# One recurrent layer and two feed-forward layers on one core: six expert units chosen from 13 tiles, then a straight list of units or the general ones

## The chip, the cores and the metric

One core of one Trainium2 chip runs the whole program; seven cores are idle. The time is the device time of one execution in microseconds (us), the median of the runs shown. Beside it stands one profiled execution with a trace of every instruction on the engines: TensorE (PE, its weight loads PEld), VectorE (DVE), ScalarE (ACT), GpSimd (POOL), and SyncE (SP), which here only issues DMAs.

## The reference

Three stages follow each other (batch 4, 8 heads, 768 steps, head size 40, so 3072 tokens of 320 numbers):

```python
# 1 mLSTM per head, with gates i, f and a sigmoid gate o
C = f_stab*C + i_stab*v k^T;  n = f_stab*n + i_stab*k
y = sigmoid(o) * (C q) / max(|n.q|, 1)
# 2 dense feed-forward, d_ff 1024
h = x @ w_in;  u = h*softmax(h);  x = layernorm(u)*g_ln @ w_out
# 3 mixture of 8 experts, one expert per token
logits = x @ w_gate + modality_bias[modality_id]; e = argmax(logits)
out = softmax(logits)[e] * (relu(x @ w1[e]) @ w2[e])      # w1 320x1024, w2 1024x320
```

The routing of the given inputs follows from the reference alone: expert 2 gets 1454 tokens, expert 4 gets 1545, expert 0 gets 73, the others none. Of the first 13 tiles of 128 tokens in the kernel's order, 803 tokens go to expert 2 and 827 to expert 4.

## The kernel before, in words

The tokens are cut into 24 tiles of 128 (chunk c of batch b). A step is a small function that issues the instructions of one thing for one tile: `score`, `pmul`, `mix_x` and their neighbours are the recurrent layer in chunks; `xs_p` and `xs_e` turn a tile's result; `ff_mm` multiplies by `w_in` into one PSUM tile `h` (a single buffer of two banks); `ff_max`, `ff_exp`, `ff_u`, `ff_sq`, `ff_r`, `ff_y`, `ff_yl` are the softmax gate and the norm; `proj` multiplies by `w_out` and the gate weights; `rows` writes the tile's 128 rows to a DRAM table. `r1a`, `r1b`, `r2`, `r3` route a group of tiles: small VectorE operations, a rank by matmul (`rk`), and one indirect DMA per tile that puts the token numbers into the lists of their experts.

The lists are cut into units. A full unit is 256 tokens of one expert, a half unit at most 128. `table_a`, `table_w`, `table_get`, `table_b` choose the expert and list rows of the next units on the chip. For unit j, `fetch_w j 0` and `fetch_w j 1` gather the expert's f32 weights (1.57 and 1.31 MB) into one of two staging sets (j mod 2); where unit j-2 had the same expert the gather's rows are out of bounds and nothing moves, though the instruction is still issued. `stat_a`, `stat_d`, `scale`, `scale2` find a scale from the sum of squares; `s1h`, `s1l`, `s2h`, `s2l` split the scaled weights into high and low f16 halves in one of two sets `w16` (j mod 2). `fetch_x` gathers and transposes the tokens; `h j 0..3` are 64 matmuls (`hp`) in four quarters, each followed by `hh` on ScalarE and `hl` on VectorE; `po j 0..1` are 48 matmuls; `ob` scales and scatters 128 rows to the output. `hs`, `hsh`, `hsl` are the same for a half unit. Every unit goes through stat, scale and split, also where the expert is that of unit j-2.

The order of the work is written out by hand: `MAIN` is one list of steps, and each engine issues its part in exactly that order, so an engine that waits holds all that stands behind it. `MAIN` ends within unit 2 and the preparation of units 3 to 5. Two units are chosen when 18 tiles are routed, two when 22 are, the rest at the end. From unit 3 on the lists `PAIR`, `HALF`, `HALF_AHEAD`, `LAST_PAIR` and `LAST_HALF` are played for each unit; from unit 8 on they stand in nested `tc.If` blocks over two counts read from SBUF into registers. There PE, ACT and DVE are in written order, POOL and SP are ordered by the framework. For these inputs there are 12 full units (six of expert 2, then six of expert 4) and two halves.

Of the kernel before, what the change touches and what calls it, by code (L numbers as in the profile page):

```python
# [48 lines left out]
def _steps(text):  # L49
    steps = [step.split() for step in text.split(",")]  # L50
    return [(name, *map(int, args)) for name, *args in steps]

# [42 lines left out]
    mix_c 11, xs_e 8, load_ea 12, scale_q 12, ff_sq 7, ff_r 7, load_a 14, proj 6, rows 6, score 13, pmul 13 0,  # L95
    ff_y 7, ff_yl 7, k_t 15, k_e 15, norm_t 9, norm_d 9, r1b 0, decay 14, norm_x 9, load_ea 13, decay_c 13,
    mix_e 11, pmul 13 1, scale_v 13, ff_mm 8 0, ff_mm 8 1, ff_max 8, ff_exp 8, mix_c 10, load_kv 17, r2 0,
    proj 7, load_a 15, xs_p 9, ff_u 8, decay_exp 14, load_kv 16, score 14, decay_c 12, mix_x 12, rows 7,
    xs_e 9, ff_mm 9 0, ff_sq 8, ff_r 8, ff_y 8, decay_c 14, ff_yl 8, scale_v 14, mix_c 14, ff_mm 9 1, ff_max 9,
    scale_q 13, ff_exp 9, scale_v 12, mix_c 12, pmul 14 0, mix_c 13, decay 15, ff_u 9, r3 0, load_a 16, k_t 16,  # L100
    k_e 16, pmul 14 1, norm_t 10, norm_d 10, proj 8, mix_e 12, mix_x 13, score 15, ff_sq 9, ff_r 9, load_kv 18,
    rows 8, decay_exp 15, scale_v 15, load_ea 15, norm_x 10, xs_p 10, load_a 17, ff_y 9, pmul 15 0, ff_yl 9,
    k_t 17, k_e 17, norm_t 11, decay 16, xs_e 10, ff_mm 10 0, ff_mm 10 1, norm_d 11, mix_e 13, pmul 15 1,
    norm_x 11, ff_max 10, decay_exp 16, load_ea 18, do_sig 2, xs_p 11, xs_e 11, decay_c 15, scale_q 15,
    ff_exp 10, mix_x 14, load_ea 17, scale_v 16, mix_c 15, score 16, ff_u 10, ff_sq 10, decay 17, pmul 16 0,
    pmul 16 1, k_t 18, k_e 18, ff_r 10, load_ea 16, load_kv 19, proj 9, rows 9, decay_c 18, ff_y 10,
    decay_c 16, ff_yl 10, norm_t 12, norm_d 12, ff_mm 11 0, ff_mm 11 1, ff_max 11, norm_x 12, decay_c 17,
    mix_e 14, mix_x 15, load_a 18, decay_exp 17, scale_v 17, scale_q 17, score 17, ff_exp 11, ff_u 11, k_t 19,
    k_e 19, pmul 17 0, ff_sq 11, ff_r 11, xs_p 12, proj 10, xs_e 12, load_kv 20, ff_y 11, ff_yl 11, scale_q 16,
    load_a 19, rows 10, decay 18, norm_t 13, norm_d 13, norm_x 13, ff_mm 12 0, ff_mm 12 1, ff_max 12, mix_e 15,  # L110
    mix_x 16, pmul 17 1, mix_c 16, ff_exp 12, ff_u 12, decay_exp 18, scale_v 18, score 18, pmul 18 0, ff_sq 12,
    load_kv 21, pmul 18 1, xs_p 13, xs_e 13, scale_q 18, k_t 20, decay 19, k_e 20, ff_r 12, proj 11, rows 11,
    norm_t 14, norm_d 14, norm_x 14, ff_y 12, ff_yl 12, ff_mm 13 0, ff_mm 13 1, ff_max 13, xs_p 14, mix_c 17,
    load_a 20, mix_e 16, mix_x 17, decay_c 3, decay_exp 19, scale_v 19, xs_e 14, score 19, k_t 21, ff_exp 13,
    ff_u 13, proj 12, decay 20, pmul 19 0, pmul 19 1, ff_sq 13, ff_r 13, r1a 1, decay_c 21, k_e 21, load_kv 22,
    norm_t 15, ff_y 13, rows 12, load_ea 19, ff_yl 13, load_a 21, ff_mm 14 0, mix_e 17, norm_d 15, load_ea 20,
    ff_mm 14 1, ff_max 14, decay_exp 20, norm_x 15, score 20, mix_x 18, pmul 20 0, decay_c 23, scale_q 19,
    ff_exp 14, ff_u 14, mix_c 18, load_kv 23, pmul 20 1, decay 21, xs_p 15, xs_e 15, proj 13, ff_sq 14,
    ff_r 14, ff_mm 15 0, k_t 22, scale_q 20, rows 13, ff_y 14, ff_mm 15 1, mix_c 21, r1b 1, k_e 22, ff_yl 14,
    ff_max 15, norm_t 16, score 21, mix_e 18, norm_d 16, norm_x 16, ff_exp 15, mix_x 19, decay_exp 21,  # L120
    load_a 22, ff_u 15, load_sig 3, decay 22, pmul 21 0, xs_p 16, pmul 21 1, ff_sq 15, ff_r 15, k_t 23,
    xs_e 16, proj 14, ff_y 15, k_e 23, ff_yl 15, rows 14, norm_t 17, norm_d 17, ff_mm 16 0, mix_e 19, r2 1,
    norm_x 17, ff_mm 16 1, ff_max 16, norm_t 18, xs_p 17, do_sig 3, norm_d 18, norm_x 18, ff_exp 16,
    load_ea 21, xs_e 17, load_ea 22, proj 15, rows 15, load_a 23, norm_t 19, norm_d 19, scale_q 21, norm_x 19,
    decay_exp 22, mix_x 20, score 22, ff_u 16, pmul 22 0, pmul 22 1, scale_q 22, mix_e 20, norm_t 20,
    norm_d 20, ff_sq 16, ff_r 16, mix_x 21, mix_e 21, decay 23, norm_x 20, ff_mm 17 0, ff_y 16, ff_yl 16,
    norm_t 21, norm_d 21, decay_c 19, ff_mm 17 1, ff_max 17, xs_p 18, norm_x 21, xs_e 18, ff_exp 17, ff_u 17,
    r3 1, mix_x 22, mix_e 22, mix_c 19, decay_exp 23, score 23, pmul 23 0, xs_p 19, ff_sq 17, pmul 23 1,
    ff_mm 18 0, ff_mm 18 1, load_ea 23, scale_q 23, ff_r 17, xs_e 19, ff_max 18, ff_y 17, ff_exp 18, ff_yl 17,
    proj 16, ff_u 18, rows 16, ff_sq 18, xs_p 20, ff_mm 19 0, ff_r 18, ff_y 18, r1a 2, ff_yl 18, proj 17,  # L130
    rows 17, ff_mm 19 1, ff_max 19, decay_c 20, mix_x 23, mix_e 23, ff_exp 19, r1b 2, ff_u 19, norm_t 22,
    norm_d 22, proj 18, scale_q 3, xs_e 20, ff_mm 20 0, rows 18, r2 2, ff_mm 20 1, ff_sq 19, ff_r 19,
    ff_max 20, norm_x 22, xs_p 21, xs_e 21, ff_exp 20, ff_u 20, norm_t 23, ff_y 19, ff_yl 19, r3 2, ff_mm 21 0,
    ff_sq 20, ff_mm 21 1, ff_r 20, table_a 0, table_w 0, fetch_w 0 1, ff_max 21, norm_d 23, ff_y 20, ff_exp 21,
    ff_yl 20, fetch_w 0 0, xs_p 22, ff_u 21, xs_e 22, norm_x 23, ff_sq 21, ff_r 21, ff_mm 22 0, table_get 0,
    a_close, stat_a 0 1, fetch_w 1 0, r1a 3, ff_mm 22 1, ff_max 22, xs_p 23, decay_c 2, xs_e 23, mix_c 20,
    proj 19, stat_d 0 1, stat_d 0 0, ff_exp 22, stat_a 0 0, table_b 0, scale 0, ff_y 21, ff_yl 21, fetch_x 0,
    fetch_x 1, rows 19, s2h 0 1, s2l 0 1, scale2 0, s1h 0 2, s1l 0 2, s1h 0 0, s1h 0 1, ff_u 22, s2h 0 0,
# [1157 lines left out]
```

## Time and profile before

| | us |
|---|---|
| median of 3 runs (666.19, 670.79, 671.93) | 670.79 |
| profiled execution, its own time | 671.24 |
| span from its first to its last instruction | 669.4 |

| engine | busy us | share of the span | instructions |
|---|---|---|---|
| PE | 541.0 | 81% | 4367 |
| DVE | 514.4 | 77% | 1097 |
| ACT | 373.2 | 56% | 570 |
| POOL | 362.8 | 54% | 334 |

The span has three stretches: the recurrent and feed-forward tiles together (until about 361 us), the last feed-forward tiles alone (until about 414 us), and the expert units. A row of the timeline is: start in us, length in us, engine, line, operation, output tile <- input tiles, count; in brackets the idle time of the engine before it and what ended it.

### The profile page before, as it was taken

The numbers are of one execution on the slowest core, as the hardware profiler recorded it, in microseconds if no ns is written. First come the engines' busy times: TensorE is split into PE (matmuls) and PEld (weight loads), VectorE is DVE, ScalarE is ACT, GpSimd is POOL, SyncE is SP. The second block draws the span as 40 slices with busy tenths as digits, with TensorE's granted clock in tenths as the row PEclk, the third lists the DMA queues.
The fourth block names the chain that finished last, engine by engine and source line by source line (L and its number), as shares of the span: only waits on it lengthen the run. The fifth ranks groups of instructions, "written<-read, shape, count | busy, mean of one in ns | idle before, by whom it ended". The sixth has DMA issues, their size and how long they took to land.

```text
span 669.4 us, 12026 instructions
## 1 busy us (share of the span) xinstructions
PE 541.0 (81%) x4367; PEld 422.5 (63%) x4367; DVE 514.4 (77%) x1097; ACT 373.2 (56%) x570; POOL 362.8 (54%) x334
## 2 busy tenths in 40 slices
...
GB/s 216 143 215 158 162 203 14 136 171 153 186 166 156 99 193 171 131 151 181 92 64 45 207 240 125 52 83 56 104 111 254 189 60 51 84 213 87 69 13 2
DMA packets 126261, 87.07 MB, mean 130 GB/s; under 512 B 106415, under 2 KB 113177, under 8 KB 124904
## 3 DMA queue, kind: packets, MB, share of 16 engines
...
q10 hardware_dynamic: 1584, 5.77, 3.0%
...
## 4 chain that ended last, share of the span: by engine, by line
PE 33%; DVE 25%; DMA 14%; ACT 11%; issue 9%; POOL 5%; DVEq 0%; ACTq 0%; POOLq 0%
PE h L683 7%; DMA out<-ob,idc 5%; DMA stg<-in_wx,wii 4%; DVE w L1077 4%; ACT w L1070 3%; PE hp L1113 3%; PE xt L596 3%; PE s L575 2%; DMA raw<-in_w_out 2%; PE dp L529 2%; DVE w L1093 2%; DVE jkd L1048 2%; PE xt L600 2%; DVE yl L725 2%; PE po L739 2%
## 5 line engine op out<-in xcount | busy, mean ns | idle before, releaser
L1113 PE MATMUL hp<-xT,w 128*128 128x256 f16 x768 | 94.6, 285 | 1.6 <-DVE w L1077 1.6
L1113 PEld LDWEIGHTS <-w 128*128 128x128 f16 x768 | 78.7, 104 | 14.5 <-DVE w L1077 2.1
L683 PE MATMUL h<-win,xh 128*128 128x512 f32 x240 | 73.1, 438 | 7.1 <-DVE e L698 6.4
L1077 DVE SCALAR_TENSOR_TENSOR w<-stg,esc,w 128x1024 f16<-128x1024 f32 (+1 forms) x42 | 65.7, 1571 | 4.8 <-ACT w L1070 3.7
L1159 PE MATMUL po<-w,hl 128*128 128x320 f16 x192 | 57.5, 299 | 9.2 <-DVE hl L1125 9.0
L1070 ACT ACTIVATE w<-stg,esc 128x1024 f16<-128x1024 f32 x42 | 47.2, 1142 | 23.7 <-DVE esc L233 23.7
L739 PE MATMUL po<-woh,yhT 128*128 128x328 f16 x192 | 55.4, 309 | 4.9 <-DVE rowb L753 3.0
L683 PEld LDWEIGHTS h<-win,xh 128*128 128x128 f32 x240 | 47.1, 207 | 18.9 <-issue 6.4
L1158 PE MATMUL po<-w,hh 128*128 128x320 f16 x192 | 57.4, 299 | 1.7 <-POOL w L1099 1.6
L1157 PE MATMUL po<-w,hh 128*128 128x320 f16 x192 | 57.5, 300 | 0.1
L642 POOL TENSOR_TENSOR sig<-sig,den 128x320 f32<-128x320 f32 x24 | 20.4, 851 | 65.1 <-DVE den L640 57.6
L740 PE MATMUL po<-wol,yhT 128*128 128x328 f16 x192 | 55.3, 308 | 0.0
L1165 POOL DMA_INDIRECT out<-ob,idc x26 | 37.1, 1427 | 30.9 <-ACT ob L1164 16.0
...
L692 ACT ACTIVATE e<-h,nm 128x1024 f32<-128x1024 f32 x24 | 26.7, 1113 | 39.7 <-DVE nm L688 39.6
L542 POOL TENSOR_TENSOR abc<-abc,gcol 128x1024 f32<-128x1024 f32 x20 | 38.5, 1926 | 16.5 <-DMA abc<-a_dram 16.5
L1005 POOL DMA_INDIRECT stg<-in_wx,wii x30 | 36.1, 1202 | 20.7 <-ACT jka L1044 3.8
...
L1044 ACT ACTIVATE jka<-stg 128x2048 bf16<-128x2048 f32 (+1 forms) x24 | 40.7, 1694 | 7.0 <-DMA stg<-in_wx,wii 6.7
L683 PE MATMUL h<-win,xl 128*128 128x512 f32 x144 | 44.4, 419 | 0.1
L596 PE MATMUL xt<-p,va 128*41 128x128 f32 x384 | 40.8, 304 | 1.9 <-DVE p L582 1.7
L725 DVE SCALAR_TENSOR_TENSOR yl<-e,r_a,yh 128x1024 f16<-128x1024 f32 x24 | 37.3, 1555 | 5.8 <-ACT yh L718 5.8
...
## 6 DMA issues: line engine op xcount, KB each, us to landing
...
```

Source lines behind the costliest of these rows:

```text
L596: nc.tensor.matmul(xt[64 * par:64 * par + VA, j, :], va[:, 4 * par + j, :], p[:, 4 * par + j, :], start=True, stop=(c == 0))
L683: nc.tensor.matmul(h[:, f, :], xx[0:kk], win[0:kk, k, f * 512:(f + 1) * 512], start=(i == 0), stop=(i == 7))
L725: nc.vector.scalar_tensor_tensor(out=yl, in0=u_t.pop(n), scalar=r_a[:, n:n + 1], in1=yh, op0=ALU.mult, op1=ALU.subtract)
L739: nc.tensor.matmul(o, yhT[:, c, :], woh[:, c, :], start=(c == 0), stop=False)
L740: nc.tensor.matmul(o, yhT[:, c, :], wol[:, c, :], start=False, stop=False)
L1044: nc.scalar.activation(jk[0], st[:, 0:hw], AF.Square, accum_out=wsq[:, q, 0:1])
L1070: nc.scalar.activation(w[:, fs], st[:, fs], AF.Copy, scale=xbuf("esc", j, [128, 2], F32)[:, 0:1])
L1077: nc.vector.scalar_tensor_tensor(out=w[r, o], in0=st[r, fs], scalar=xbuf("esc", j, [128, 2], F32)[r, 0:1], in1=w[r, fs], op0=ALU.mult, op1 ...
L1113: nc.tensor.matmul(hp[:, f, :], w[0:kk, k * FF + fc * 128:k * FF + fc * 128 + 128], xT[0:kk, xk, :], start=(i == 0), stop=(i == 7))
L1157: nc.tensor.matmul(pq[:, 0:DM], th[:, fc, us], wh, start=(fc == 0), stop=False)
L1158: nc.tensor.matmul(pq[:, 0:DM], th[:, fc, us], wl, start=False, stop=False)
L1159: nc.tensor.matmul(pq[:, 0:DM], tl[:, fc, us], wh, start=False, stop=(fc == 7))
```

## The change

- `groups` (the tiles that are routed together) is 7, 6, 7 and 4 tiles in place of 7, 7, 4, 4, 2. `r1a 0`, `r1b 0`, `r2 0`, `r3 0` stand in a row behind `rows 6`; before, `r1a 0` stood ahead of `proj 5` and the three others were spread over the next three tiles.
- A new `table_f`, after 13 tiles are routed, takes the lowest and the highest expert that have at least 768 tokens by then, and makes units 0 to 5 of them in turn (low, high, low, high, low, high). `table_a 1` makes the other units (up to 19) at unit 3, again in turn from the front and the back of the list of full units, and `table_w` works out `go`: 1 if units 6 to 11 and 13 each have the expert of unit j-2, there are exactly six full units left and eight units in all.
- `MAIN` now holds units 0 to 5 whole. Weights are fetched and split for units 0 and 1 alone; for the others `scale3` applies the scale already found. In units 0 to 5 all four quarters of `h` take their PSUM tile from the two of `ps_h`.
- Then `go` is read into a register on every engine. Where it is 1, the list `TAIL` follows, without further branches and in written order on all five engines: units 6 to 11 without fetch or split, unit 12 fetched and split beside them, unit 13 before unit 12. Otherwise `READY` (fetch and split unit 6, fetch unit 7) and the units of before follow from unit 6.

The diff, cut to its core (in the two lists, all that concerns the units from the last tiles on):

```diff
-NPAIR = 12 + 7
-EARLY = (2, 2)
+NFAST = 6
+NREST = 12 + 7
+NPAIR = NFAST + NREST
...
-    xs_e 7, ff_sq 6, ff_r 6, r1a 0, load_kv 15, load_ea 14, ... proj 6, rows 6, score 13, pmul 13 0, ...
-    norm_d 9, r1b 0, decay 14, ... load_kv 17, r2 0, proj 7, ... ff_u 9, r3 0, load_a 16,
+    xs_e 7, ff_sq 6, ff_r 6, load_kv 15, load_ea 14, ... proj 6, rows 6, r1a 0, r1b 0, r2 0, r3 0, score 13,
...
+    r1a 1, c_units, r1b 1, score 20, ... r2 1, ff_max 14, k_t 22, table_f 0, ... table_get 0, ... table_b 0, ...
+    fetch_w 0 0, ff_sq 16, ... proj 18, rows 18, fetch_w 0 1, ff_mm 20 0,
+    ff_mm 20 1, ff_y 19, ff_yl 19, ff_max 20, norm_t 23, norm_d 23, xs_p 21, xs_e 21, norm_x 23, a_close,
+    fetch_w 1 0, ff_exp 20, ff_u 20, stat_d 0 0, xs_p 22, ff_mm 21 0, ff_mm 21 1, xs_e 22, stat_d 0 1,
+    decay_c 23, stat_a 0 1, ff_sq 20, ff_r 20, proj 19, stat_a 0 0, ff_y 20, ff_max 21, ff_yl 20, ff_exp 21,
+    ff_u 21, fetch_x 0, xs_p 23, rows 19, ff_sq 21, r1b 2, xs_e 23, stat_a 1 0, ff_mm 22 0, ff_r 21, ff_y 21,
+    ff_mm 22 1, ff_max 22, ff_yl 21, ff_exp 22, ff_u 22, fetch_x 1, proj 20, rows 20, ff_sq 22, scale 0,
+    ff_mm 23 0, s1h 0 1, ff_r 22, ff_y 22, r2 2, ff_mm 23 1, ff_max 23, ff_exp 23, s1l 0 1, ff_yl 22, proj 21,
+    rows 21, stat_d 1 0, s1h 0 2, s1h 0 0, s1l 0 0, fetch_w 1 1, s1l 0 2, h 0 0, stat_d 1 1, ff_u 23, s2h 0 1,
+    s2l 0 1, stat_a 1 1, ff_sq 23, ff_r 23, hh 0 0, hl 0 0, h 0 2, scale 1, ff_y 23, ff_yl 23, h 0 3, scale2 1,
+    hh 0 3, hl 0 3, s1h 1 1, s1l 1 1, proj 22, s2h 0 0, s1h 1 0, rows 22, h 0 1, hh 0 1, hl 0 1, s2h 1 1,
+    scale2 0, hh 0 2, proj 23, s2l 0 0, rows 23, hl 0 2, po 0 0, s1l 1 0, scale3 4, s1h 1 2, s1l 1 2, ob 0 0,
+    s2h 1 0, po 0 1, s2l 1 1, fetch_x 2, scale3 3, ob 0 1, h 1 0, hh 1 0, hl 1 0, h 1 1, hh 1 1, hl 1 1,
+    s2l 1 0, h 1 3, hh 1 3, hl 1 3, h 1 2, hh 1 2, hl 1 2, r3 2, po 1 0, ob 1 0, fetch_x 3, r1a 3, po 1 1,
+    ob 1 1, scale3 2, h 2 0, r1b 3, r2 3, r3 3, h 2 1, hh 2 0, hl 2 0, ...
+    po 3 0, table_a 1, ob 3 0, h 4 0, hh 4 0, po 3 1, hl 4 0, table_w 1, table_get 1, ob 3 1, h 4 1, table_b 1, ...
+TAIL = _steps("""
+    scale3 8, h 6 3, scale3 9, h 6 0, scale3 6, hh 6 0, h 6 1, hh 6 1, scale3 7, hh 6 3, hl 6 0, fetch_w 12 1,
+    hl 6 1, h 6 2, hh 6 2, hl 6 2, fetch_w 12 0, hl 6 3, po 6 0, ob 6 0, fetch_x 8, po 6 1, ob 6 1, h 7 0, ...
+    po 11 1, ob 11 1, s2l 12 0, hs 13 0, hs 13 1, hsh 13 0, hsl 13 0, hsh 13 1, hsl 13 1, s1h 12 0,
+    s1l 12 0, scale3 13, po 13 0, ob 13 0, hs 12 0, hs 12 1, hsh 12 0, hsl 12 0, hsh 12 1, hsl 12 1, po 12 0,
+    ob 12 0
+""")
...
+    def scale3(j):
+        einv = xbuf("einv", j, [128, 2], F32)
+        nc.vector.tensor_scalar(out=P2["gat"][:, 2 * j:2 * j + 2], in0=P2["gat"][:, 2 * j:2 * j + 2],
+                                scalar1=einv[:, 0:1], scalar2=einv[:, 1:2], op0=ALU.mult, op1=ALU.mult)
...
-        if f2 < 2 or j < 2:
+        if f2 < 2 or j < NFAST:
             hp = P2['ps_h'].tile([128, 2, 256], F32, tag="hp", name=f"hp{j}_{f2}")
...
+    play(MAIN)
+    at = saved()
+    straight = nc.values_load(P2["go"][0:1, 0:1], min_val=0, max_val=1)
+    with tc.If(straight > 0) as cmp:
+        play(TAIL)
+    with cmp.Else():
+        restore(at)
+        general(NFAST)
```

## Rows read from the trace of the kernel before

**Rows 1.** Page, part 1: busy us (share of the span) and instructions of each engine.

```profile
PE 541.0 (81%) x4367; PEld 422.5 (63%) x4367; DVE 514.4 (77%) x1097; ACT 373.2 (56%) x570; POOL 362.8 (54%) x334
```

**Rows 2.** Windows: stretch, length, then busy us of PE, PEld, DVE, ACT, POOL, granted clock, DMA.

```profile
250.00:300.00 50.00, 47.42 (x440) 37.83 (x436) 42.45 (x98) 23.82 (x40) 25.08 (x25) 1.00 0.69 156
...
540.00:560.00 20.00, 17.98 (x146) 13.83 (x144) 19.02 (x25) 17.05 (x20) 12.73 (x9) 1.00 0.27 62
```

**Rows 3.** Groups by line, DVE, 500 to 600 us (busy us, mean ns | idle before).

```profile
L1077 DVE SCALAR_TENSOR_TENSOR w<-stg,esc,w 128x1024 f16<-128x1024 f32 (+1 forms) x19 | 32.2, 1693 | 2.8 <-ACT w L1070 2.1
L1093 DVE SCALAR_TENSOR_TENSOR w<-stg,esc,w 128x1792 f16<-128x1792 f32 x7 | 18.7, 2675 | 0.0
L1125 DVE SCALAR_TENSOR_TENSOR hl<-hp,hh 128x512 f16<-128x512 f32 x27 | 18.6, 687 | 1.0
L1048 DVE SCALAR_TENSOR_TENSOR jkd<-stg 128x1024 bf16<-128x1024 f32 x12 | 16.1, 1341 | 0.2
```

**Rows 4.** Timeline, PE, unit stage: unit 3's first quarter, unit 3's second `po` matmul on.

```profile
480.58 2.00 PE L1113 MATMUL hp<-xT,w 128*128 128x256 f16 x16
...
492.56 0.30 PE L1158 MATMUL po<-w,hh 128*128 128x320 f16 x1 [1.58 <-POOL w L1099]
...
498.94 1.91 PE L1113 MATMUL hp<-xT,w 128*128 128x256 f16 x16
...
500.84 5.40 PE L1113 MATMUL hp<-xT,w 128*128 128x256 f16 x48
...
628.03 1.99 PE L1135 MATMUL hs<-xT,w 128*128 128x128 f16 x32 [1.00 <-SPq L1230]
```

**Rows 5.** Timeline, PE, from the end of `ff_mm 20` to unit 1.

```profile
360.26 0.87 PE L683 MATMUL h<-win,xl 128*128 128x512 f32 x3
...
387.99 0.40 PE L1000 MATMUL pi<-ident,idg 4*128 4x4 f32 x2 [3.44 <-DVE idg L997]
...
392.06 0.43 PE L739 MATMUL po<-woh,yhT 128*128 128x328 f16 x1 [3.02 <-DVE rowb L753]
...
400.38 0.86 PE L683 MATMUL h<-win,xl 128*128 128x512 f32 x3
...
413.38 0.59 PE L1054 MATMUL pw<-wsq,onef 128*128 128x4 f32 x2 [8.78 <-ACT w L1044]
...
435.95 3.66 PE L1113 MATMUL hp<-xT,w 128*128 128x256 f16 x32
```

**Rows 6.** Chain of waits, 370 to 436 us: start, length, what.

```profile
374.94 11.61 DMA stg<-in_wx,wii
...
395.41 16.32 DMA stg<-in_wx,wii
```

**Rows 7.** Timeline, DVE: one each of `ff_max`, `ff_yl`, `s1l`.

```profile
361.18 1.23 DVE L688 TENSOR_REDUCE nm<-h 128x1 f32<-128x1024 f32 x1 [0.25 <-PE h L683]
...
364.82 1.35 DVE L725 SCALAR_TENSOR_TENSOR yl<-e,r_a,yh 128x1024 f16<-128x1024 f32 x1
...
399.65 1.28 DVE L1077 SCALAR_TENSOR_TENSOR w<-stg,esc,w 128x1024 f16<-128x1024 f32 x1
```

**Rows 8.** Timeline, DVE and PE: `r1a 0` (first and last of 22); PE behind `proj 6`.

```profile
180.37 0.69 DVE L778 TENSOR_SCALAR rt<-se_a 128x7 f32<-128x7 f32 x1
...
185.07 0.17 DVE L794 TENSOR_TENSOR rt<-rt,rt 128x7 f32<-128x7 f32 x1
...
195.81 1.16 PE L575 MATMUL s<-qk,kT 40*128 40x128 f32 x16
...
205.53 0.67 PE L619 MATMUL dc<-wv,kpad 128*64 128x41 f32 x16 [2.89 <-DVE xn L647]
```

**Rows 9.** Timeline, PE, last half unit; then PE's branches of line 1215 (ns min/median/max).

```profile
644.77 5.38 PE L1135 MATMUL hs<-xT,w 128*128 128x128 f16 x64 [5.70 <-issue]
...
653.11 0.30 PE L1159 MATMUL po<-w,shl 128*128 128x320 f16 x1
...
L1215 PEldq COMPARE_BRANCH  x9: 65/190/2907, 559.1 to 625.0; - x9
```

More of the change, by code (lines that the diff above doesn't have):

```diff
@@ L94 @@
     mix_x 11, decay_exp 12, pmul 12 0, scale_v 11, ff_exp 7, ff_u 7, scale_q 14, pmul 12 1, decay_exp 13,
[L95 to L138, printed above, removed]
@@ L139 @@
-    s2l 0 0, proj 20, rows 20, ff_sq 22, ff_r 22, stat_a 1 0, s1l 0 1, ff_mm 23 0, fetch_w 1 1, ff_mm 23 1,
-    ff_max 23, ff_exp 23, stat_d 1 0, s1l 0 0, proj 21, stat_d 1 1, stat_a 1 1, ff_u 23, ff_y 22, scale 1,
-    scale2 1, h 0 0, hh 0 0, ff_yl 22, hl 0 0, ff_sq 23, ff_r 23, h 0 1, hh 0 1, hl 0 1, rows 21, r1b 3, h 0 3,
-    h 0 2, s2h 1 0, r2 3, table_a 1, ff_y 23, proj 22, s2h 1 1, rows 22, r3 3, table_w 1, fetch_w 2 0, hh 0 2,
-    hl 0 2, hh 0 3, hl 0 3, po 0 1, s1h 1 1, s1h 1 0, s1l 1 0, po 0 0, s1l 1 1, s1h 1 2, s1l 1 2, ff_yl 23,
@@ L149 @@
[L149 to L152 removed]
+    mix_c 11, xs_e 8, load_ea 12, scale_q 12, ff_sq 7, ff_r 7, load_a 14, proj 6, rows 6, r1a 0, r1b 0, r2 0,
@@ new lines @@
+    decay 17, pmul 16 0, pmul 16 1, k_t 18, k_e 18, ff_r 10, load_ea 16, load_kv 19, proj 9, rows 9,
+    decay_c 18, ff_y 10, decay_c 16, ff_yl 10, norm_t 12, norm_d 12, ff_mm 11 0, ff_mm 11 1, ff_max 11,
+    norm_x 12, decay_c 17, mix_e 14, mix_x 15, load_a 18, decay_exp 17, scale_v 17, scale_q 17, score 17,
+    ff_exp 11, ff_u 11, k_t 19, k_e 19, pmul 17 0, ff_sq 11, ff_r 11, xs_p 12, proj 10, xs_e 12, load_kv 20,
+    ff_y 11, ff_yl 11, scale_q 16, load_a 19, rows 10, decay 18, norm_t 13, norm_d 13, norm_x 13, ff_mm 12 0,
```

310 lines of the change are left out of this document (206 added, 104 removed).

## The prediction, before the result was known

> **What bounds the kernel now.** I read the page first. PE is busy 81% of the span and DVE 77% [rows 1], so neither is the bound throughout, and the stretches decide. The windows show two regimes [rows 2]. From 250 to 300 us PE works 47.4 of 50 us beside 42.5 of DVE: PE's order sets the pace. In the unit stage (540 to 560) both are nearly full, DVE with 19.0 of 20 us. Next I read the groups of DVE there [rows 3]: over 100 us it spends 32.2 and 18.7 us on splitting weights and 16.1 us on sums of squares, but 18.6 us on `hl`, the only group that a unit needs if its weights are there already. So 67 us of each 100 go into preparing weights, mostly of an expert that was prepared before. The timeline of PE [rows 4] shows what that costs: units 3 to 11 start at 480.58 and the first half unit at 628.03, 147.5 us for nine units, 16.4 each. PE's own work is less. A quarter of `hp` (16 matmuls) runs from 498.94 to the next instruction at about 500.69, 0.109 us a matmul, and 47 `po` matmuls from 492.56 to 498.94, 0.136 each; so a full unit is 64 x 0.109 + 48 x 0.136 = 7.0 + 6.5 = 13.5 us. Last I read PE between the last feed-forward tiles and unit 1 [rows 5]. `ff_mm 20` ends at 361.1, `ff_mm 23` only at 401.2: 40 us for three tiles, with PE held 3.4 us by the list of units 0 and 1 and 3.0 us behind their preparation. Then it idles 8.8 us until the weights of unit 1 have landed; the chain of waits shows why, a load of 16.3 us [rows 6]. Unit 1 starts at 435.95.
>
> **The change part by part.** For these inputs both large experts have 768 tokens after 13 tiles (803 and 827), and the rest is 3 + 3 full units and two halves, so `go` is 1 and the straight list is played. I sum along PE, against the profiled execution (671.24, 0.45 above the median; span 669.4, 1.84 around it).
>
> *Routing of the first seven tiles.* Behind `proj 6` PE now goes on at once (195.81). After the change its next instruction is the rank of `r2 0`, which waits for `rows 6`, all of `r1a 0` (22 instructions in 4.9 us, 0.22 each) and ten of `r1b 0` at 0.22: at least 7.1 us idle. A wait of 2.9 us that PE has at 205.53 behind this same work goes [rows 8]. Net +4, and it stays, since PE is the bound in the tiles that follow [rows 2]. Ends: 0 (the 4.9 us that DVE no longer spends earlier come back) and +8 (nothing does). On POOL the seven puts of `r3 0` are moved ahead of `norm_d 9` and `decay 14`; before, they stood ahead of `norm_t 10`. What could be late behind them is `norm_x 9`; that lies inside the same ends. So `ff_mm 20` ends at 365.
>
> *The last three tiles.* The in-order waits for the unit list go, as that list is read at tile 16. DVE's list sets the pace: per tile `ff_max` and `ff_u` 1.23 each, `ff_yl` 1.35 [rows 7], `xl` 0.5 (by columns), `ff_r` and `rows` seven small instructions at 0.22; 5.9, for three tiles 17.7. Beside them two `stat_d` 2.5, `r1b 2` and `r2 2` 4.4, `scale 0` 1.3, the norm of tile 23 about 1, and some 2.5 of waits for ACT and POOL: 29.4 us until `ff_mm 23` ends, where it was 40.1. Then DVE needs `ff_max`, three `s1l` at 1.28, `ff_yl`, `rows`, one `stat_d`, 8.3 us, with a hop 9.5, before `h 0 0` can start, 38.9 after `ff_mm 20` (52.7 before). `fetch_w 1 1` is queued on POOL behind `fetch_x 1`, which waits until `rows 19` is in DRAM, so I put its issue at +23; at 11.6 to 16.3 us a load [rows 6] it lands at +35 to +39, just when `stat_d 1 1` comes up. Cost 0; if that cover is gone, `ff_u 23` and with it `proj 23` wait behind `stat_d 1 1`, and the old 8.8 us are the far end.
>
> *Unit 0.* 7.0 of `hp`, two `proj` of 24 matmuls at 0.136 (6.6) and 6.5 of `po` are 20.1; 3.6 more for `h 0 3` behind `hl 0 0` and `proj 23` behind its transposes. Unit 1 starts 62.6 after `ff_mm 20`, at 427.6, where it was 435.95 with one `proj` still to come.
>
> *Units 1 to 11.* Fetch, sums, scale and split go from ten units, POOL's part of the split too, and 24 of 30 fetches, 20 of them empty; DVE is left with four `hl` at 0.69, 2.8 us a unit. PE becomes the bound: 13.5 and 0.3 for waits on a quarter's PSUM tile, 13.8 x 11 = 151.8. Units 2 and 4 get +5: in unit 2 the rank waits for `r1a 3` and `r1b 3`, in unit 4 some 35 instructions of `table_a 1` (7.7 us at 0.22) run beside 8.3 us of PE's work, and then `pi` waits for the list to land. POOL's seven puts of `r3 2` delay `ob 1 0` and `fetch_x 3`, whose tokens are due a unit later. `fetch_w 12` stands ahead of `fetch_x 8` on POOL's queue; two loads of 11.6 fit into the two units (27 us) before unit 8. Unit 11 ends at 584.4.
>
> *The branch.* PE's branches at line 1215 took 0.065, 0.19 (median) and up to 2.9 us [rows 9]. I take 0.2, as the list follows the branch in the code; ends 0 and 2.9. The Trainium skill ("Runtime: NRT & Kernel Launch", Instruction fetch mechanics) says that prefetch is sequential and that a taken branch to a page not held waits for that page. By that rule, were `TAIL` the target, the sum would take the far end, 621.
>
> *Halves and end.* `hs` is 0.062 a matmul [rows 4], 4.0 for 64, and `po` 3.3: 14.5 for both, with 1.0 for the last `s1l` of unit 12. That is 15.5, where 628.03 to 653.4 was 25.4, of it 5.7 for a branch [rows 9]. PE ends at 600.1. The 16.0 us from PE's last matmul to the end of the span I keep: 616.1. With 1.84 around it: **618 us**.
>
> **The rivals.**
> *The pace does not follow PE.* Something beside the weights sets it: the two PSUM tiles of units 0 to 5, the scatters, the gathers. Then units run at some 15.3, half way between 13.8 and 16.4 and a little over: 11 x 1.5 = +16, 634. For it: POOL keeps four indirect DMAs a unit in order. Against: the gaps in [rows 3] and [rows 4] end on weights, at a POOL or ACT instruction of the split.
> *No earlier start.* POOL brings the second half of unit 1's weights late again, or DVE's list is longer than I count: +10, 628; with the first rival 645.
> *It goes better.* The routing burst is absorbed and the waits in units 0 to 4 vanish: 608.
> *The straight list is not taken* (the change does not do what it says), and this one is slower than before. It decides where `go` is 0, one count off six or eight or one `same` short. Unit 6 would start at 427.6 + 5 x 13.8 + 5 = 501.6, and then four loads are fetched with nothing beside them. At 11.6 for a pair in flight four take 23 to 46 [rows 6]; 27, near the lower end, as no transposes compete. With sums (2 x 1.34) and three splits at 1.7 [rows 3] +35; six units at 16.4 = 98.4; halves and end as before 25.4 + 16.0 + 1.8: 678. Against it: the counts above. The Trainium skill ("DMA: Bandwidth & Descriptors", Anatomy of one DMA, SWDGE path) fits a DMA of this kind with 2.0 us plus its bytes over 436 GB/s. By that the 5.77 MB take an estimated 15.2 us, and this rival ends at 666, no change; the loads shown [rows 6] were longer, so I keep 678.
>
> **How the numbers follow.** Forecast 618 (610 to 627 by itself) 0.50; pace 634, 0.18; late start 628, 0.16; both 645, 0.04; better 608, 0.08; straight list not taken 678, 0.03; 0.01 for something else near no change. A measurement of this kernel tells about 1% from no change, 6.7 us: faster is under 664.1, slower over 677.5. Faster 0.95, same 0.02, slower 0.03. The range 604 to 640 takes in the forecast, both single rivals and the better case.
>
> **What would show it.** After the change: nine to ten units at 13.6 to 14 us between first quarters; three `s1l` after unit 1 (unit 12's) where there were 36; no 8.8 us wait at `pw`; a new wait of 7 us or more on PE behind `proj 6`; PE's clock at 1.00 through the units; one half unit straight after the other. Wrong would be: 14 units each with their splits (`go` is 0), a DVE still full beside the units, or units that wait for gathers.

## The result: 611.9 us against 671.4 us

The changed kernel took 611.93 us (median of 4 runs, 611.27 to 615.11), the kernel before 671.36 us beside it (4 runs, 666.19 to 672.88). The ratio is estimated at 0.914, with a 95% interval of 0.9095 to 0.9186. Here and below, medians and ratios leave out executions that took over 1.5% longer than the fastest of the same kernel on its chip. The forecast was 618 us, its range 604 to 640: the mechanism held, and the sum was six microseconds too long, with larger errors in both directions behind it. The profiled execution took 615.11 us, its span 613.4.

I cut both spans along TensorE at the points that the prediction used. "Forecast" is the length that the prediction gave to the stretch.

| stretch, us | before | forecast | after |
|---|---|---|---|
| start to the end of `ff_mm 20` | 361.1 | 365.0 | 374.8 |
| to the end of `ff_mm 23` | 40.1 | 29.4 | 25.7 |
| to `h 0 0` | 12.6 | 9.5 | 6.0 |
| to unit 1 | 22.1 | 23.7 | 25.1 |
| units 1 to 11, to the first half unit | 192.1 | 157.0 | 156.1 |
| the two halves, to the end of PE | 25.4 | 15.5 | 13.8 |
| to the end of the span | 16.0 | 16.0 | 11.9 |

Of the 56.0 us gained in the span, 36.0 are the units, 21.0 the two stretches behind `ff_mm 20`, 15.7 the halves and the end; 13.7 are lost ahead of `ff_mm 20`, and 3.0 in unit 0.

### The profile page after: what moved, and what is told of

Its sections match the earlier page's. It is cut to its first block, busy times and chain, and to the rows that moved or that the text cites. A ratio compares the mean times of both kernels' runs of the same rounds, so it can differ in the third digit from the quotient of the medians.

```text
span 613.4 us, 11412 instructions
## 1 busy us (share of the span) xinstructions
PE 530.7 (87%) x4338; PEld 420.3 (69%) x4338; DVE 370.8 (60%) x889; ACT 275.9 (45%) x470; POOL 273.1 (45%) x290
## 5 line engine op out<-in xcount | busy, mean ns | idle before, releaser
L1194 PE MATMUL hp<-xT,w 128*128 128x256 f16 x768 | 91.0, 280 | 8.8 <-DMA xT<-xg 3.8
L1194 PEld LDWEIGHTS <-w 128*128 128x128 f16 x768 | 76.6, 101 | 21.2 <-issue 4.3
L1206 DVE SCALAR_TENSOR_TENSOR hl<-hp,hh 128x512 f16<-128x512 f32 x48 | 32.5, 689 | 92.5 <-ACT hh L1202 92.3
L1246 POOL DMA_INDIRECT out<-ob,idc x26 | 27.1, 1042 | 120.0 <-ACT ob L1245 100.6
L727 PEld LDWEIGHTS h<-win,xh 128*128 128x128 f32 x240 | 46.4, 203 | 15.1 <-DVE e L742 3.8
L1202 ACT ACTIVATE hh<-hp 128x512 f16<-128x512 f32 x48 | 28.1, 595 | 57.2 <-PE hp L1194 57.2
L1245 ACT ACTIVATE ob<-po,gat 128x320 f32<-128x320 f32 x26 | 13.7, 528 | 62.2 <-PE po L1240 52.5
L1097 POOL DMA_INDIRECT xg<-x_dram,idc x28 | 29.7, 1062 | 20.7 <-DMA x_dram<-rowb 10.9
L626 DVE TENSOR_TENSOR p<-s,abc 128x512 f32<-128x512 f32 x48 | 31.6, 681 | 9.7 <-PE s L619 9.6
L769 DVE SCALAR_TENSOR_TENSOR yl<-e,r_a,yh 128x1024 f16<-128x1024 f32 x24 | 33.9, 1413 | 4.9 <-ACT yh L762 3.6
L732 DVE TENSOR_REDUCE nm<-h 128x1 f32<-128x1024 f32 x24 | 29.3, 1221 | 9.8 <-PE h L727 9.6
```

Source lines behind the costliest of these rows:

```text
L626: nc.vector.tensor_tensor(out=p_t[n][:, gs, :], in0=ps_t.pop((n, g)), in1=abc_t[n][:, gs, :], op=ALU.mult)
L727: nc.tensor.matmul(h[:, f, :], xx[0:kk], win[0:kk, k, f * 512:(f + 1) * 512], start=(i == 0), stop=(i == 7))
L769: nc.vector.scalar_tensor_tensor(out=yl, in0=u_t.pop(n), scalar=r_a[:, n:n + 1], in1=yh, op0=ALU.mult, op1=ALU.subtract)
L1194: nc.tensor.matmul(hp[:, f, :], w[0:kk, k * FF + fc * 128:k * FF + fc * 128 + 128], xT[0:kk, xk, :], start=(i == 0), stop=(i == 7))
L1206: nc.vector.scalar_tensor_tensor(out=hx_t[j][1][:, sl, :], in0=hp_t.pop((j, f2)), scalar=0.0, in1=hx_t[j][0][:, sl, :], op0=ALU.max, op1=A ...
```

## The profile after

Busy time of the whole span; this answers to [rows 1]:

```profile
span 613.4 us, 11412 instructions
...
PE 530.7 (87%) x4338; PEld 420.3 (69%) x4338; DVE 370.8 (60%) x889; ACT 275.9 (45%) x470; POOL 273.1 (45%) x290
```

The two windows of [rows 2], columns as there:

```profile
250.00:300.00 50.00, 49.63 (x463) 39.65 (x461) 36.49 (x91) 27.51 (x44) 26.38 (x29) 1.00 0.69 158
540.00:560.00 20.00, 20.00 (x164) 15.73 (x162) 5.87 (x10) 4.51 (x9) 5.14 (x5) 1.00 0.32 81
```

In the unit stage PE is now busy all 20 us and DVE 5.87, where it was 19.0. DVE's groups from 500 to 600 us say why; they answer to [rows 3]:

```profile
L1206 DVE SCALAR_TENSOR_TENSOR hl<-hp,hh 128x512 f16<-128x512 f32 x26 | 17.3, 689 | 56.1 <-ACT hh L1202 56.1
L1158 DVE SCALAR_TENSOR_TENSOR w<-stg,esc,w 128x1024 f16<-128x1024 f32 (+1 forms) x3 | 4.0, 1327 | 2.4 <-ACT w L1151 2.4
```

`hl` has nearly the same count (26, before 27) and the same size as before; of the 19 splits of the first matrix three are left, those of unit 12. TensorE's timeline from unit 0 to the first half unit answers to [rows 4, 5] (start, length, ..., in brackets the idle time before; the rows at 463.14 and 587.69 are cut short by the window that was asked for):

```profile
406.50 0.61 PE L1194 MATMUL hp<-xT,w 128*128 128x256 f16 x2 [2.60 <-ACT w L1151]
409.12 5.41 PE L1194 MATMUL hp<-xT,w 128*128 128x256 f16 x30 [2.01 <-DVE w L1158]
...
431.59 7.15 PE L1194 MATMUL hp<-xT,w 128*128 128x256 f16 x64
...
463.14 1.03 PE L1194 MATMUL hp<-xT,w 128*128 128x256 f16 x8 [3.79 <-DMA xT<-xg]
...
506.51 7.15 PE L1194 MATMUL hp<-xT,w 128*128 128x256 f16 x64
...
520.02 7.15 PE L1194 MATMUL hp<-xT,w 128*128 128x256 f16 x64
...
587.69 0.50 PE L1216 MATMUL hs<-xT,w 128*128 128x128 f16 x6
```

Unit 6 starts at 506.51 and unit 7 at 520.02, 13.5 us apart, and each `hp` is one piece of 64 matmuls without a gap. There are two things to see ahead of that: unit 0 starts with two waits for its own split, and unit 3 waits 3.79 us for its tokens. The routing block is in the same view (POOL, DVE and PE):

```profile
204.56 0.21 PE L870 MATMUL rk<-oh,upper 128*128 128x64 f16 x1 [7.94 <-DVE oh L861]
...
204.92 2.08 PE L619 MATMUL s<-qk,kT 40*128 40x128 f32 x16
...
206.66 1.21 POOL L896 DMA_INDIRECT ids_dram<-tokid,pi  x1 [8.67 <-DVE pi L889]
...
215.16 0.97 POOL L896 DMA_INDIRECT ids_dram<-tokid,pi  x1 [0.31 <-issue]
216.15 0.74 POOL L686 TENSOR_TENSOR sig<-sig,den 128x320 f32<-128x320 f32 x1
...
216.92 0.49 DVE L691 TENSOR_TENSOR xn<-tr,sig 128x320 f32<-128x320 f32 x1 [6.42 <-POOL sig L686]
...
217.56 0.67 PE L663 MATMUL dc<-wv,kpad 128*64 128x41 f32 x16 [3.03 <-DVE xn L691]
```

PE waits 7.94 us for the rank, and the matmuls behind this wait are slow: the 16 of `s` take 2.08 us, which took 1.16 at 195.81 in [rows 8]. A window from 204.5 to 211.8 us shows a granted clock of 0.50 (the 1.2 GHz level), where the clock had been 1.00 before the wait. Then the seven puts hold POOL from 206.66 to 216.13; `norm_d 9`'s multiplication (`sig`) stands behind them, DVE waits 6.42 us for that, and PE 3.03 us for `norm_x 9`.

## Experiments

Three groups were run, each group on one chip with the kernel before beside it (681.36, 666.20 and 672.39 us there); the changed kernel itself stood in the second and the third, as `c1_after` and `c2_after`. Unless the text says otherwise a kernel is held against those.

### What routing the first group in one block costs

`e1_spread`, and the same kernel again as `e1_again`:

```diff
-    xs_e 7, ff_sq 6, ff_r 6, load_kv 15, ... rows 6, r1a 0, r1b 0, r2 0, r3 0, score 13, ...
+    xs_e 7, ff_sq 6, ff_r 6, r1a 0, load_kv 15, ... rows 6, score 13, ... norm_d 9, r1b 0, ...
+    load_kv 17, r2 0, ... ff_u 9, r3 0, ...
```

`e2_puts` moves `r3 0` alone behind `ff_u 9`.

> The changed kernel with the four routing steps of the first group (r1a 0, r1b 0, r2 0, r3 0) back at the places that they had before, the rest as changed. Theory: of the 13.7 us by which ff_mm 20 ends later than before (374.8 against 361.1), nearly all comes from routing this group in one block, by the 7.9 us wait of PE for the rank and the 3.0 us wait behind the puts. Then ff_mm 20 ends at 361 to 365 and the time is 600 to 603 us. Rival: the burst is caught up by tile 13 and the new order of tiles 14 to 20 is what costs; then ff_mm 20 ends at 371 or later and the time is 609 to 613 us.

> The changed kernel with only the seven puts r3 0 back at their place before (behind ff_u 9); the rest of the block stays behind rows 6. Theory: the puts hold POOL from 206.7 to 216.1 and norm_d 9's multiplication on POOL behind them, DVE waits 6.4 us for that, PE 3.0 us, and a matmul of the proj that follows takes twice its time; so this alone is worth 4 to 6 us: 606 to 608 us, while PE's wait of 7.9 us for the rank stays. Rival: the whole loss is the rank's wait, and norm 9 is late behind DVE's block anyway: 611 to 613 us.

> The first group's routing back at its places of before, once more, now beside the changed kernel on the same chip. From the first measurement (ff_mm 20 ends 202 us after ff_mm 6 starts, 204 in the changed kernel, 193 before): theory, the block costs only what is not caught up later, 2 to 4 us, and the rest of the 13.7 us lies in the new order of tiles 8 to 20: ratio to the changed kernel 0.993 to 0.997. Rival: the late semaphores hid the gain, and without them it is 9 to 13 us: ratio 0.979 to 0.986.

> The changed kernel itself, unchanged, as the one that the others of this group are held against. In the runs of the first group the four kernels' updates of TensorE's semaphore came up to 18 us late while the puts of a routed group were under way, which the first trace of the changed kernel does not show. If that belongs to the chip or the hour and not to the edits, this run shows it too where the group's other runs do, and its ratio to the kernel before is again 0.91 to 0.92; if the edits brought it, this run has every update within 0.3 us of its instruction's end.

In the first group `e1_spread` took 611.53 us (ratio to before 0.8976, 0.8891 to 0.9060) and `e2_puts` 617.24 (0.9058, 0.8964 to 0.9151): the rival's number, and neither's. That group's traces have the late updates that the last section tells of, and the changed kernel did not run in it, so I ran the first kernel again beside the changed one: 602.72 us against 613.40 (ratios to before 0.9032, 0.8829 to 0.9234, and 0.9185, 0.9062 to 0.9309), 10.7 us less. No wait ended on a late update in either of these two. `e1_again` came out as its rival said; the guess that the block costs only 2 to 4 us was wrong. Its windows from the start of `ff_mm 6` to the end of `ff_mm 8`, of `ff_mm 10` and of `ff_mm 20` show it; first the kernel before, then the changed kernel (first trace), then `e1_again`:

```profile
168.00:202.60 34.60, 32.44 (x277) 24.86 (x274) 28.90 (x74) 17.40 (x29) 19.77 (x18) 1.00 0.72 175
202.60:237.70 35.10, 27.19 (x273) 20.62 (x273) 25.33 (x62) 16.20 (x26) 23.49 (x26) 1.00 0.66 127
237.70:361.10 123.40, 115.97 (x1042) 91.11 (x1040) 98.75 (x261) 66.58 (x110) 58.42 (x60) 1.00 0.61 134
```

```profile
170.40:214.50 44.10, 35.39 (x284) 27.59 (x282) 28.99 (x91) 18.14 (x31) 23.73 (x22) 0.88 0.59 139
214.50:250.60 36.10, 29.39 (x265) 21.96 (x265) 19.88 (x44) 15.52 (x25) 20.93 (x24) 0.91 0.72 145
250.60:374.80 124.20, 117.05 (x1038) 92.69 (x1036) 96.55 (x276) 67.49 (x110) 60.19 (x65) 0.99 0.62 150
```

```profile
166.50:201.00 34.50, 32.48 (x277) 24.86 (x275) 28.73 (x76) 17.40 (x29) 20.32 (x19) 1.00 0.74 177
201.00:237.70 36.70, 30.70 (x272) 23.12 (x273) 24.22 (x61) 16.30 (x27) 23.84 (x27) 0.86 0.63 130
237.70:362.40 124.70, 118.32 (x1037) 93.14 (x1036) 96.64 (x276) 67.20 (x110) 60.24 (x65) 0.97 0.64 153
```

The first two of these stretches in `c1_after`, which shares a chip with `e1_again`:

```profile
169.10:214.10 45.00, 36.33 (x285) 28.30 (x282) 28.72 (x91) 18.12 (x31) 24.34 (x23) 0.85 0.57 137
214.10:247.70 33.60, 27.77 (x264) 21.40 (x265) 19.93 (x44) 15.53 (x25) 20.34 (x23) 0.95 0.74 157
```

Read the lengths: the first stretch takes 34.6, 44.1 and 34.5 us, and 45.0 in `c1_after`. The block costs 9.5 to 10.5 us where it stands, and spreading it gives that back. PE's timelines add the 9.5 up: 7.94 for the rank's wait, 2.8 for the matmuls behind it at the lower clock (the granted clock of the stretch is 0.88 against 1.00), 0.4 for the rank's own matmuls, less 1.5 for two waits at 188.42 and 189.30 that the changed kernel does not have. In the first trace nothing of it is caught up in the tiles that follow. In `c1_after` 3.1 us are: its second stretch takes 33.6 us against 36.7 in `e1_again`, which has its low clock there (0.86). From `ff_mm 6` to `ff_mm 20` it is 202.8 against 195.9 us, so 6.9 remain; the kernel before took 193.1, so 2.8 belong to the other new orders. `e2_puts` still waits 8.07 us for the rank and takes 45.1 us in the first stretch. PE no longer waits for `norm_x 9` there, but the first two stretches take 78.1 us, against 78.6 in `c1_after`, so its theory fell: the puts alone are worth little. The traces of `c1_after` and `e1_again` lie 13.7 us apart (the medians 10.7): 6.9 in these stretches, 2.6 ahead of them, where runs differ (`ff_mm 6` began at 164 to 170 us), and 4.2 in the units.

### The tokens of unit 3

`e3_late_puts` moves `r3 2` from ahead of `po 1 0` to behind `fetch_x 3`.

> The changed kernel with the seven puts r3 2 behind fetch_x 3 instead of ahead of it. Theory: PE's wait of 3.8 us at unit 3 for its tokens is the price of these puts on POOL's queue; it goes and all that follows moves up: 608 us. Rival: the tokens wait for the queue of transposes or for the traffic of the puts, which stays; the wait is then 3 us or more again, in unit 3 or as a wait of unit 2 or 4: 611 to 613 us.

It took 627.23 us (0.9175, 0.9070 to 0.9280), neither theory's number. PE does not wait at unit 3, but 5.76 and 10.73 us in unit 2, which the last section takes up; so the run doesn't settle what the puts' place is worth. `e8_late_group` below moved them as well, in a group without late updates, and there PE waits for tokens 2.2 us in all, nowhere at unit 3. In the changed kernel the gathers of unit 3 landed 6.5 and 5.7 us after their issue at 446.4 and 447.8, those of unit 5, with no puts ahead of them, after 3.1 us. So the puts delay the gathers behind them twice: they hold POOL (from 435.58 to 444.82), and gathers that are issued while puts are under way land later.

But the traces show that this is not what PE waits for at unit 3. The gathered tokens are transposed by two more DMAs. The second one of unit 3 was issued at 454.23, and its last update came at 463.00, 8.8 us later; the second one of unit 4, issued at 468.57, took 3.4 us. With 3.4 us unit 3 would have had its tokens before PE was ready for it at 459.35. `c1_after` shows the same (issued at 451.60, 9.8 us; PE waits 5.2 us). In `e1_again` this transpose took 4.9 us and PE waits nowhere at unit 3; its 2.2 us are a wait at unit 4, whose gathers stand behind the puts of `r3 3`. What held the one transpose up, with the same order of puts in all three, stays open.

### The straight list

`e4_general` makes the test for the straight list fail, so the general units follow unit 5.

```diff
-        v.tensor_scalar(out=P2["go"], in0=cum[:, 2 * NE - 1:2 * NE], scalar1=8.0, scalar2=b, ...
+        v.tensor_scalar(out=P2["go"], in0=cum[:, 2 * NE - 1:2 * NE], scalar1=9.0, scalar2=b, ...
```

> The changed kernel with one constant of its test for the straight list made unreachable (nine units in all where eight are counted), so that the general units follow unit 5. It computes the same. By the mechanism of my rival (four weight loads with nothing beside them 27 us, sums and splits 8 us, six units at 16.4 us, halves and end 43 us) on this kernel's own start of unit 6 at 506.5: 683 us. With the loads at an estimated 15.2 us, by the Trainium skill (DMA: Bandwidth & Descriptors, Anatomy of one DMA, SWDGE path): 671 us. If the straight list is worth nothing but its order, units at 13.5 us would go on after the loads and the time is 655 us or less.

Measured: 671.87 us (2 runs; 0.9847, 0.9704 to 0.9989), some 58 us over the changed kernel of the two other groups. The prediction's rival had 678 and the expectation 683, but not by a working that the trace bears out. The rival's largest term was four weight loads, 27 us. The chain of waits and PE's timeline at the start of unit 6:

```profile
500.33 4.71 DMA out<-ob,idc
...
509.22 2.11 DMA stg<-in_wx,wii
```

```profile
515.01 0.59 PE L1130 MATMUL pw<-wsq,onef 128*128 128x4 f32 x2 [12.32 <-ACT jka L1120]
517.86 0.39 PE L1194 MATMUL hp<-xT,w 128*128 128x256 f16 x1 [2.25 <-ACT w L1151]
...
521.95 3.17 PE L1194 MATMUL hp<-xT,w 128*128 128x256 f16 x14 [2.66 <-DVE w L1158]
```

The load took 2.11 us: units 4 and 5 hold the same two experts, so the rows are out of bounds and nothing moves. PE's wait of 12.32 us runs through the landing of unit 5's last scatter, the branch, this empty load and the sums of squares; then come the scale and the split, and unit 6 itself takes 25.5 us. From PE's last matmul of unit 5 (502.7) to unit 7 that is 27 us over a plain unit, where the rival had 35 for loads, sums and splits. The units from 6 to 10 take 17.4 us in the mean (517.9 to 604.9), but 25.5, 14.4, 14.4, 19.2 and 13.6 one by one. The Trainium skill's figure ("DMA: Bandwidth & Descriptors", Anatomy of one DMA, SWDGE path) gave 671, as measured, by chance: no weights were moved here for its figure to be tested on.

### What held a unit at 16.4 us

`e5_resplit` puts sums, scale and splits back into units 6 to 10 of the straight list, from the staged weights and without fetches. `e6_dve_half` keeps only VectorE's share of that work, `e7_act_half` only ScalarE's and GpSimd's.

```diff
-    scale3 8, h 6 3, scale3 9, h 6 0, scale3 6, hh 6 0, h 6 1, ...
+    scale3 6, h 6 0, scale 7, hh 6 0, scale2 7, s1h 7 0, hl 6 0, h 6 1, hh 6 1, s1l 7 0, h 6 2, hl 6 1, s1h 7 1,
+    h 6 3, hh 6 2, s1h 7 2, hl 6 2, hh 6 3, s2h 7 1, s1l 7 2, hl 6 3, po 6 0, s2h 7 0, s1l 7 1, po 6 1,
+    stat_d 8 1, stat_d 8 0, stat_a 8 1, stat_a 8 0, s2l 7 0, s2l 7 1, fetch_x 8, ob 6 1, ob 6 0, ...
```

> The changed kernel with units 6 to 10 of the straight list in the old order for a unit: sums of squares, scale and splits of the weights of the next unit again, from the staged weights, which are still there, and no fetches. It computes the same values once more. Theory: preparing weights is what held units at 16.4 us; units 6 to 10 go from 13.5 to 15.5 to 16.5 us each, the time is 10 to 15 us longer. Rival: the pace was set by the fetches on POOL or by the branches between units, and stays 13.5 to 14.0: 0 to 3 us longer.

> As the kernel that splits again in units 6 to 10 of the straight list, but with only VectorE's part of it (three low halves of w1, one of w2, its sums of squares, the scale; the third low half is a second first one, so that the values stay). Theory: it is VectorE's list that held a unit above TensorE's 13.5 us (there 13.6 us busy per 15.1 us unit); alone it takes some 12.5 us a unit, in order between the hl steps, so units 6 to 10 take 14 to 15 us and the time is 3 to 8 us over the changed kernel. Rival: it was the handing over between ScalarE, VectorE and GpSimd and their slowing each other down; with VectorE alone units take 13.5 to 13.8 us and the time is 0 to 2 us over.

> As the kernel that splits again in units 6 to 10, but with only ScalarE's and GpSimd's part of it (high halves, ScalarE's sums of squares, GpSimd's low half; the third high half is a second first one). Theory (VectorE's list holds the units): units 6 to 10 take 13.5 to 13.8 us, the time is 0 to 2 us over the changed kernel. Rival (the handing over, or ScalarE's list, in which hh waits behind a split of 1.1 to 1.8 us): 14 us a unit or more, 3 us over or more.

> The changed kernel unchanged, on the same chip as the three others of this group, so that each is held against it: 612 to 615 us.

Measured: `e5_resplit` 628.95 us, 15.6 over `c1_after`; `e6_dve_half` 620.68 and `e7_act_half` 615.29, 7.6 and 2.2 over `c2_after` (613.07). The totals mislead: in these kernels unit 12 is prepared in the old order, late, and unit 11 with what follows until `hs` takes 21.8, 21.0 and 15.2 us against 13.6 in `c2_after`. The five units themselves are told apart by a window over them: the changed kernel, both halves, VectorE's half, ScalarE's and GpSimd's half.

```profile
506.50:574.00 67.50, 67.50 (x562) 54.81 (x560) 15.91 (x26) 20.13 (x34) 22.52 (x22) 1.00 0.44 127
```

```profile
502.20:577.90 75.70, 70.63 (x572) 55.46 (x571) 66.03 (x90) 57.06 (x70) 41.67 (x28) 0.98 0.34 83
```

```profile
506.60:574.90 68.30, 68.30 (x573) 55.58 (x571) 54.49 (x90) 16.25 (x29) 26.09 (x21) 1.00 0.35 104
```

```profile
503.90:572.10 68.20, 68.20 (x572) 55.49 (x571) 22.79 (x58) 58.59 (x72) 36.53 (x30) 1.00 0.50 111
```

Both halves together take 15.1 us a unit, each alone 13.7 at most: PE stays full. So it was not VectorE's own work alone, and my theory for `e6_dve_half` fell. As many instructions of DVE, 90, take 54.49 us alone and 66.03 us beside the other half. Its groups show which grow; first `e6_dve_half`, then `e5_resplit` (518 to 573 us; the split of 64 partitions takes 1.28 us too where nothing lengthens it):

```profile
L1158 DVE SCALAR_TENSOR_TENSOR w<-stg,esc,w 128x1024 f16<-128x1024 f32 x12 | 15.3, 1277 | 0.0
L1206 DVE SCALAR_TENSOR_TENSOR hl<-hp,hh 128x512 f16<-128x512 f32 x16 | 11.0, 686 | 0.8 <-ACT hh L1202 0.8
```

```profile
L1206 DVE SCALAR_TENSOR_TENSOR hl<-hp,hh 128x512 f16<-128x512 f32 x15 | 10.3, 687 | 0.6
L1158 DVE SCALAR_TENSOR_TENSOR w<-stg,esc,w 64x1024 f16<-64x1024 f32 x4 | 8.4, 2096 | 1.4 <-ACT w L1151 1.4
```

And the timeline of `e5_resplit` shows beside what:

```profile
524.37 3.35 DVE L1158 SCALAR_TENSOR_TENSOR w<-stg,esc,w 64x1024 f16<-64x1024 f32 x1 [0.35 <-ACT w L1151]
...
525.12 1.50 POOL L1179 TENSOR_TENSOR w2s<-stg,esc 128x768 f32<-128x768 f32 x1
...
528.50 0.45 PE L1240 MATMUL po<-w,hl 128*128 128x320 f16 x1 [2.60 <-DVE hl L1206]
```

A split that takes 1.28 us alone takes 3.35 us around a multiplication of 1.50 us on GpSimd; the last `hl` of the unit stands behind it, and PE waits 2.60 us for that. `hl`, which reads PSUM and one SBUF tile, keeps its 0.69 us. In the five units eight instructions of DVE took over 0.5 us longer than in `e6_dve_half`, 10.4 us in all, and each of them had such a piece of the split on GpSimd beside it. The Trainium skill ("SBUF — State Buffer", Who interferes with whom) says that a VectorE instruction with two SBUF inputs contends with a GpSimd instruction that reads SBUF, and that one with a single SBUF input doesn't; these rows agree. A kernel that leaves out GpSimd's part alone was not run, so ScalarE's share in it is argued from the rows only: its splits took 1.14 us with and without VectorE's half. Some of the loss does not come from longer instructions. In unit 9 of `e5_resplit` every split of the first matrix took 1.28 or 1.29 us, and PE still waited 0.68 us for an `hl`; and in unit 7, behind the wait of 2.60 us, PE was busy 15.2 us, at a granted clock of 0.90, where it is 13.6. Before, a unit took 16.4 us. That is a mean over units of 13.9 to 21.7 us, and PE's waits in these nine add up to 18.8 us: 9.0 for an `hl`, the rest but for 1.0 for a sum or a split of weights. These runs do not divide the 1.3 us between 16.4 and 15.1.

### A faster version

`e8_late_group` is `e1_spread` with the third and fourth group's routing, and the second list, moved into the units; `e10_best` adds an earlier split for unit 0.

```diff
-    ... ff_r 19, r1a 2, ... ff_sq 21, r1b 2, ... ff_y 22, r2 2, ... hl 1 2, r3 2, ... fetch_x 3, r1a 3, ... r1b 3, r2 3, r3 3, ...
+    ... fetch_x 3, r1a 2, r1b 2, ... hl 2 1, r2 2, ... fetch_x 4, r3 2, hh 2 2, hl 2 2, r1a 3, r1b 3, ...
+    hl 3 1, r2 3, r3 3, ... ob 4 0, table_b 1, fetch_x 6, ...
```

```diff
-    ff_y 22, ... ff_exp 23, s1l 0 1, ff_yl 22, proj 21, rows 21, stat_d 1 0, s1h 0 2, s1h 0 0, s1l 0 0, fetch_w 1 1, s1l 0 2, h 0 0
+    ff_y 22, s1h 0 2, ... ff_exp 23, s1h 0 0, s1l 0 1, s1l 0 2, proj 21, rows 21, s1l 0 0, ff_yl 22, stat_d 1 0, fetch_w 1 1, h 0 0
```

> As the kernel with the first group's routing spread, and the third group's (r1a 2, r1b 2, r2 2, some 42 small VectorE instructions) moved from the last feed-forward tiles into units 1 and 2, the fourth group's into units 2 and 3, their puts behind them, the second list (table_b 1) behind unit 4. Theory: VectorE's list sets the pace of the last three tiles and of the start of unit 0, so taking 8.8 us of small instructions out of 365 to 401 us brings unit 1 forward by 5 to 9 us against the spread kernel, and the units, which leave VectorE idle for 14 of 20 us, take the routing for 0 to 2 us. Rival: TensorE itself is busy 22.3 of 25.7 us between ff_mm 20 and ff_mm 23, so at most 3 us come back, or the new wait for the list behind unit 4 takes them.

> As the kernel with the first group's routing spread and the third group's late, and the high halves of unit 0's w1 on ScalarE while it waits for VectorE at tile 23 (s1h 0 2 ahead of ff_exp 23, s1h 0 0 behind it), the low halves ahead of ff_yl 22 and of the sums of unit 1. Theory: of the two waits of TensorE at the start of unit 0 (2.6 us for a high half, 2.0 us for a low half) 2 to 3 us go, and unit 1 starts as much earlier: about 598 us, 2 to 3 us below the kernel without this. Rival: proj 22 and 23 then wait for the later ff_yl 22 and ff_u 23, and nothing is gained.

`e8_late_group` took 601.27 us (0.8992, 0.8859 to 0.9125), 12.1 under `c1_after`, and beats both kernels. But against `e1_again` the late routing brings only 1.5 us, within what those two vary, as its rival said. From the end of `ff_mm 20` to unit 1 are 54.8 us, 56.8 in `e1_again`. The window from `ff_mm 20` to `ff_mm 23`, first `e8_late_group`, then `e1_again`:

```profile
367.00:390.70 23.70, 20.42 (x112) 14.98 (x111) 18.04 (x44) 19.14 (x28) 8.19 (x8) 1.00 0.92 200
362.40:388.10 25.70, 22.33 (x121) 16.33 (x120) 21.51 (x64) 19.30 (x29) 7.35 (x8) 0.93 0.81 198
```

With twenty small instructions fewer on DVE it is 2.0 us shorter, but PE does not wait less: it idles 3.3 and 3.4 us. It is busy 1.9 us less, at a granted clock of 1.00 in place of 0.93 and without the rank's eight matmuls. Why the clock did not fall there is not shown. `e10_best` took 600.67 us (0.8913, 0.8839 to 0.8987), 12.4 under `c2_after`, so its own edit gains nothing that can be told. PE's first wait for the split went, and this came:

```profile
393.85 3.34 PE L1194 MATMUL hp<-xT,w 128*128 128x256 f16 x29 [1.79 <-DVE w L1158]
...
401.77 3.57 PE L1194 MATMUL hp<-xT,w 128*128 128x256 f16 x16 [3.99 <-DVE hl L1206]
```

DVE comes to the first `hl` 36.9 us after `ff_mm 20`, where it was 37.3 in `e8_late_group`, and `h 0 3` waits 3.99 us for its PSUM tile. Unit 1 starts 57.0 us after `ff_mm 20`.

## Why the prediction was right, step by step

- **What bounds it: right.** PE sets the pace of the units once the preparation is gone. The reason was half right: I read a DVE with 67 of 100 us of preparation as a full engine. Its own instructions would have fitted; beside GpSimd's share of the split they are longer (54.5 and 66.0 us for 90). The sign was in the prediction's own rows: the splits of the first matrix took 1.69 us in the mean in [rows 3], the one in [rows 7] 1.28.
- **Routing of the first seven tiles: the term that was mis-sized**, 4 us forecast, 9.5 measured. The rank's wait was sized right (at least 7.1, measured 7.94). Two steps failed. One is that PE's old wait of 2.9 us [rows 8] goes and leaves nothing. It did come from the routing: before, `norm_x 9` (`xn`) stood on DVE right behind `r1b 0`, which starts at 200.04.

```profile
200.04 0.18 DVE L802 TENSOR_SCALAR rt<-rt,wsi 128x7 f32<-128x7 f32 x1
...
204.90 0.48 DVE L647 TENSOR_TENSOR xn<-tr,sig 128x320 f32<-128x320 f32 x1
```

Now it stands behind the seven puts and costs PE 3.03 us. The prediction saw that `norm_x 9` could be late and gave it no time of its own. The other is the granted clock of 0.50 behind the rank's wait, 2.8 us, for which the sum had no term. That the loss stays until the units was right for this trace; in `c1_after` 3.1 of 10.5 us came back. The rest of the 13.7 us is 2.4 at the start of `ff_mm 6` and 1.8 in the two later windows.
- **The last three tiles and the start:** 29.4 and 9.5 forecast, 25.7 and 6.0 measured. I took DVE's list for the bound and added it up to 29.4, but DVE was busy 21.5 of the 25.7 us and PE 22.3. And I put three low halves ahead of `h 0 0`; it starts on the high halves, and the last low half is the 2.01 us wait within it.
- **`fetch_w 1 1` at no cost: right.** Issued 21.4 us after `ff_mm 20` (at 396.23), landed in 10.0 us at 406.24, and `stat_d 1 1` starts at 409.10. Unit 0 took 25.1 us, 23.7 forecast.
- **Units 1 to 11: the sum right (156.1, forecast 156.8), its parts not.** A unit has no 0.3 us of PSUM waits (13.5 flat). The losses in units 1 to 4 were 7.6 us, not 5. Of these, 3.8 are the wait for unit 3's tokens and 1.7 the lower clock behind it: unit 3's 64 `hp` took 8.81 us where other units take 7.15. Neither was in the sum. That the puts' delay of `fetch_x 3` has a unit to spare was right; it was the transpose behind that came late. PE waited 0.23 us at most for the rank and `table_a 1`. That the sum came out is luck.
- **The branch at 0.2 us: right.** No wait stands between unit 5 and unit 6 on PE. The rule of the Trainium skill that I cited ("Runtime: NRT & Kernel Launch", Instruction fetch mechanics) would have made 621 if the list had been the target of a taken branch and not yet held. No run shows whether it was; the stall did not come.
- **Halves and end:** 13.8 and 11.9 against 15.5 and 16.0. PE did not wait for unit 12's last split. The end is shorter on POOL's queue. Before, a join of the branches stood there between the last scatter and the drain, and the drain took 9.1 us; now there is no join, and the drain takes 7.2. First the kernel before, then the changed kernel (ns min/median/max):

```profile
L1230 POOLq INC_SWDGE_SEM  x1: 2415/2415/2415, 656.8 to 656.8; - x1
```

```profile
L1398 POOLq DRAIN  x3: 107/192/7168, 604.9 to 613.0; - x3
```

The terms behind `ff_mm 20` were 12.5 us too long together, those ahead of it 9.8 too short; that makes 618 against the profiled 615.1. That the two nearly cancel is luck. The median lies 3.2 us below the profiled execution.
